# Reading the chunk state of a gated linear attention over all 112 rows at once, on one core

## The chip, the cores and the metric

One core of a Trainium2 chip runs the whole program. The metric is the device time of one execution in microseconds (us). The engines are named as in the profile: PE (matrix multiply), PEld (its weight loads), DVE (vector), ACT (scalar), POOL and SP (which here issues DMAs).

## The reference, cut to what matters

```
q, k, v, alpha: 4 batches x 8 heads x 768 tokens x 48, float32
state[d,e] = alpha_t[d] * state[d,e] + k_t[d] * v_t[e]        (per batch and head)
y_t[e]     = sum_d q_t[d] * state[d,e]
x   = y with the heads side by side: 4 x 768 x 384
u   = x + real(fft over tokens and over columns of x)
un  = layer norm of u over its 384 columns
out = u + relu(un @ w_ch1) @ w_ch2                            (384 -> 1536 -> 384)
```

## The kernel before

The recurrence is computed in chunks of 128 tokens, six to a sequence, and two heads at a time: a **pair** (16 of them, four to a batch). Within a pair the rows (partitions) 0 to 47 hold the 48 state rows of the first head and rows 64 to 111 those of the second; rows 48 to 63 are padding, so a pair takes 112 rows (`CW`). `HEADS` gives the two row slices, 0:64 and 64:112.

`attn_stages` writes the work of one pair as stages. s1 to s3 form running products of alpha and the scaled k and q on DVE. s4 transposes k on PE. s5 multiplies scaled q with scaled k per chunk and head on PE, with operands of 64 rows (first head) and 48 rows (second head), ACT copies the results out and POOL masks them; the result is `X`. s6 makes the contribution of each of the first five chunks to the state (`pu`, on PE), and DVE turns it into the state before each later chunk: one tensor_tensor over 112 x 240, then four dependent scalar_tensor_tensor of 112 x 48. They write the tile `tt`, one of two that alternate between pairs.

s7 makes the output of the six chunks. For chunk cc there is, for each head, a matmul of `X` with the values `vn` (128 rows; 64 streamed columns, of which 48 are used), called **V** here, and for cc > 0 a matmul of `e["A"]` with the state, called **T** here, which adds to the same columns. T runs over rows 0:64 for the first head and 64:112 for the second, with 48 streamed columns each. Each head has a PSUM bank of its own (`py[hd]`) for all six chunks; after chunks 2 and 5, ACT copies the three finished chunks of each head out (`FL["ev"].copy`, 128 x 144, four per pair). A matmul of plain float32 operands shows as two instructions in the trace (the 160 calls of T stand there as 320), one of the fp32r type as one.

After s7 the batch is combined over tokens, mixed by Fourier matrices, normed, and goes through the two layers of 384 -> 1536 -> 384, the **F** matmuls here (fp32r, 128 rows, 384 columns; 864 of each layer). The attention of batch b+1 is interleaved with the F matmuls of batch b. Batch 0's attention has no such work beside it.

The order on every engine is fixed ahead by a planner, `Plan.emit` (from line 363): it gives each operation a duration (`duration`), starts it when its inputs are ready by that account (matmuls other than F wait 0.8 us more, `MARGIN`), and takes, among what can start, what has the lowest key. PE executes strictly in the planned order. PSUM has eight banks: three "a" (attention and mixing), two "f1" and three "f2" (F matmuls); batch 0's attention may use all eight.

Up to a planned time of 120 us (`WARM`) the planner puts **fillers** into the planned gaps of PE (line 1135 in the profile): matmuls of a zero tile of 32 columns into columns 480:512 of bank 2 of "f2". It leaves them out while that bank holds an unfinished sum (`self.open`).

Of the kernel before, what the change touches and what calls it, by code (L numbers as in the profile page):

```python
# [17 lines left out]
ALU = mybir.AluOpType  # L18
AX = mybir.AxisListType

B, H, S, D = 4, 8, 768, 48
DM = H * D
DFF = 4 * DM
P = 128
NT = S // P
NP2 = H // 2
# [3 lines left out]
HM = DM // 2  # L30
CW = 112
GRP = 64
VW = NT * H // NP2 * D + GRP - D
VROW = 640
EVAC = 5000.0
NY = 5
# [17 lines left out]
KCK = -700.0  # L54
KF0 = -505.0
WARM = 120.0
MARGIN = 0.8
DUMMY = 0.11
KTINY = 0.5 * 2.0**15 / (1.0 + 15.5 / 128.0)
# [39 lines left out]
HEADS = ((0, slice(0, GRP)), (1, slice(GRP, CW)))  # L99
# [78 lines left out]
class Plan:  # L178


    def __init__(self, engines):
        self.engines, self.ops, self.tags, self.direct, self.key, self.chain, self.fill = engines, [], {}, None, 0.0, None, False
        self.idle, self.open, self.both, self.half = None, False, None, None

    def tag(self, name, count, make):
        reals = [make(i) for i in range(count)]
# [176 lines left out]
    def emit(self):  # L363
# [5 lines left out]
        clock = {e: 0.0 for e in self.engines}  # L369
# [6 lines left out]
        order = []  # L376
# [22 lines left out]
        while placed < len(ops):  # L399
            placed += 1  # L400
            best = None
            for e, cand in wait.items():
                if not cand:
                    continue
                now = clock[e]
                times = []
                for n in cand:
                    op = ops[n]
                    t = start(op, e)
                    if t is None:  # L410
                        continue
                    if len(op.engines) > 1:
                        if any(finish(op, o) < finish(op, e) - SLACK[e] for o in op.engines if o != e):
                            continue
                    times.append((t, max(now, t), n))
                if not times:
                    continue
                first = min(x[1] for x in times)
                key, n, t = min((ops[n].key, n, max(t, now)) for t, late, n in times if late <= first + WINDOW[e])
                if best is None or t < best[0]:  # L420
                    best = (t, n, e)
            assert best is not None, "no instruction can be placed"
            t, n, engine = best
            op = ops[n]
            for e in op.engines:
                wait[e].remove(n)
            op.engine, op.dur = engine, op.durs[engine]
            if engine == "PE":
                if op.half is not None and self.half is not None and op.half != self.half:
                    op.dur, self.half = 0.04, None  # L430
                else:
                    self.half = op.half
            for slot in op.slots:
                if slot.tag and slot.cell is None:
                    tag = self.tags[slot.tag]
                    slot.cell = tag["free"].pop(0)[1]
                    tag["taken"].add(slot.index)
                    while tag["next"] in tag["taken"]:
                        tag["next"] += 1
            if op.engine == "PE" and self.idle and t < self.idle[2] and not self.open:  # L440
                for _ in range(int((t - max(clock["PE"], self.idle[1])) / DUMMY)):
                    order.append(self.idle[0])
            if op.name == "matmul" and self.idle and (op.args[0].tile.tag, op.args[0].tile.cell) == self.idle[3]:
                self.open = not op.kwargs["stop"]
            if op.port and op.engine in held:
                op.dur += max(0.0, held[other[op.engine]] - t)
                held[op.engine] = t + op.dur
            end = t + op.dur
            clock[op.engine] = end
            if "dma" in op.name:  # L450
                dge = max(dge, t) + 0.45
                wire = max(wire, dge + 0.6) + op.wire
                end = wire + 1.0
            op.t, op.end = t, end
            order.append(n)
            for slot in op.slots:
                slot.touched.append(end)
                if slot.tag and len(slot.touched) == slot.uses:
                    tag = self.tags[slot.tag]
                    tag["free"].append((max(slot.touched) + 0.2, slot.cell))  # L460
                    tag["free"].sort(key=lambda x: x[0])
            for m in op.users:
                u = ops[m]
                u.left -= 1
                for e in u.engines:
                    lat = 0.0 if "dma" in op.name else LAT[op.engine][e]
                    if e == "PE" and op.engine != "PE" and not u.fill:
                        lat += MARGIN
                    u.ready[e] = max(u.ready[e], t if u.behind == n else end + lat)
                    if not u.left:  # L470
                        wait[e].append(m)
        self.order = [n for n in order if isinstance(n, int)]
        for n in order:
# [3 lines left out]
            op = ops[n]  # L477
# [21 lines left out]
def gla_mix_ffn(ctx: ExitStack, tc: tile.TileContext, alpha, kq, v, w1, w2, consts, rowtab, out):  # L499
    nc = tc.nc  # L500
    plan = Plan({"PE": nc.tensor, "ACT": nc.scalar, "DVE": nc.vector, "POOL": nc.gpsimd, "SP": nc.sync})
# [33 lines left out]
    def psa():  # L535
        if state["start"]:
            state["i"] += 1
            return plan.tile(start_tags[state["i"] % 8])
        return plan.tile("a")
# [8 lines left out]
    def fixed(shape, name, dtype=F32):  # L548
        return plan.fixed(cp.tile(shape, dtype, name=name))
# [3 lines left out]
    ident = cst[:, ID_O : ID_O + P]  # L553
    wts = [None] * (NW // 2)
    loaded = {}
    tts = [fixed([P, NT - 1, D], f"tt{i}") for i in range(2)]
    mts = [fixed([P, NT], f"mt{i}") for i in range(3)]
    d1 = fixed([P, S], "d1")
    back = fixed([P, S], "back")
# [4 lines left out]
    zero = fixed([P, 32], "zero")  # L564
# [47 lines left out]
    def setup():  # L612
        V.memset(zero, 0.0)
        V.memset(d1, 0.0)
        V.memset(back, 0.0)
        V.memset(back[:, C - 1 :: 2 * C], 1.0)
        V.memset(cm63, -63.0)
        V.memset(ceps, 1e-6)
        for x in mts:
            V.memset(x, 0.0)  # L620
        V.memset(ones, 1.0)
        V.memset(bad, 0.0)
# [40 lines left out]


    def attn_stages(b, hp, i, mixed):
        tt, mt = tts[i], mts[hp % 3]
        pair = b * NP2 + hp
        e = {}
        halves = "p (c h t) -> p c h t"
# [78 lines left out]
        def s6():  # L748
            pu = psa()
            for a in range(NT - 1):  # L750
                for hd, r in HEADS:
                    T.matmul(
                        pu[r, a * D : (a + 1) * D], e["kt"][:, a, r], loaded["vn", pair][:, (2 * a + hd) * D : (2 * a + hd + 1) * D],
                        start=True, stop=True,
                    )
            V.tensor_tensor(
                out=tt[0:CW], in0=pu[0:CW, 0 : (NT - 1) * D].rearrange("p (a e) -> p a e", e=D),
                in1=mt[0:CW, 0 : NT - 1, None].broadcast_to([CW, NT - 1, D]), op=ALU.mult,
            )
            for a in range(1, NT - 1):  # L760
                V.scalar_tensor_tensor(
                    out=tt[0:CW, a], in0=tt[0:CW, a - 1], scalar=mt[0:CW, a : a + 1], in1=tt[0:CW, a], op0=ALU.mult, op1=ALU.add,
                )

        def s7():
            X = e["X"]
            ytiles = mixed()[0]
            py = [psa() for _ in HEADS]
            for h2 in range(2):
                for c in range(3):  # L770
                    cc = 3 * h2 + c
                    cs = slice(cc * P, (cc + 1) * P)
                    o = cc * GRP
                    for hd, _ in HEADS:
                        T.matmul(
                            py[hd][:, o : o + GRP], X[h2][:, hd, c], loaded["vn", pair][:, (2 * cc + hd) * D : (2 * cc + hd) * D + GRP],
                            start=True, stop=cc == 0,
                        )
                    for hd, r in HEADS if cc else ():
                        T.matmul(py[hd][:, o : o + D], e["A"][r, cs], tt[r, cc - 1], start=False, stop=True)  # L780
                for hd, _ in HEADS:
                    yo = py[hd][:, 3 * h2 * GRP : 3 * (h2 + 1) * GRP].rearrange("p (a e) -> p a e", a=3)[:, :, 0:D]
                    FL["ev"].copy(ytiles[h2][:, :, (2 * hp + hd) * D : (2 * hp + hd + 1) * D], yo)

        return [s1, s2, s3, s4, s5, s6, s7, lambda: combine(*mixed(), hp * 2 * D, 2 * D, FL["comb"])]

# [343 lines left out]
    pf = psa()  # L1130
    T.matmul(pf[0:1, 0:1], bs, ones, start=True, stop=True)
    V.tensor_scalar_min(fl, pf[0:1, 0:1], 1.0)
    warm = plan.tags["f2"]["reals"]
    if WARM:
        plan.idle = (lambda: nc.tensor.matmul(warm[2][0:32, 480:512], zero.real(), zero.real(), start=True, stop=True), 1.0, WARM, ("f2", 2))  # L1135
    with tc.manual_schedule():
        plan.emit()

# [145 lines left out]
```

## Time and profile before

| | |
|---|---|
| three runs | 570.28, 576.63, 589.35 us (median 576.63) |
| the profiled execution | 578.74 us, of which the span of the trace is 577.0 us |
| mean granted PE clock in it | 0.93 |
| busy: PE, PEld, DVE, ACT, POOL | 555.3, 515.7, 341.6, 192.1, 77.5 us |

The stages overlap. Up to about 101 us there is batch 0's attention and mixing, with the splitting of the weights on ACT and DVE; from there the F matmuls are interleaved with the attention and mixing of the next batch, and from about 448 us on almost only F matmuls are left. The last F matmul ends at 569 us.

A row of a group of instructions gives line, engine, operation, out<-in by the names of tiles, shapes, count, total busy time and mean time of one in ns. For a matmul "64*128 64x48" is the weight tile (rows * columns) and the moving tile (rows x streamed columns). The names there are those of the pools: w is `e["A"]` or X, vn the values, f and a the PSUM banks, h, x and wt operands of the F matmuls. A row of the view by stretches of time gives the stretch, its length, the busy time and number of instructions of PE, PEld, DVE, ACT and POOL in it, the mean granted PE clock, the share of the DMA engines and GB/s. Line 481 is that of the planner's emission and so says nothing of the place in the code.

### The profile page before, as it was taken

The page shows a single profiled execution, that of the slowest core. Times are in us where ns is not written, and L with a number is a line of the kernel's source. Part 1 is how long each engine was busy: PE and PEld are TensorE (multiplying, and loading weights), DVE is VectorE, ACT ScalarE, POOL GpSimd, SP SyncE. Part 2 cuts the span into 40 slices and gives each one's busy share as a digit, 9 for nine tenths or more (in the row PEclk, how much of TensorE's full clock was granted, in tenths as well). Part 3 has the DMA queues.
Part 4 walks back from the last instruction along what each step waited for, and adds up shares of the span by engine and source line. Part 5 has one row for each costly group of instructions (what it writes and reads, how often), then busy time and mean ns, then how long its engine had stood idle before and what let it go on. Part 6 is the DMA issues. An engine that isn't in the chain of part 4 may idle for free.

```text
span 577.0 us, 11019 instructions
## 1 busy us (share of the span) xinstructions
PE 555.3 (96%) x4550; PEld 515.7 (89%) x4550; DVE 341.6 (59%) x831; ACT 192.1 (33%) x425; POOL 77.5 (13%) x99
## 2 busy tenths in 40 slices
PE   6999996999999999999999999999999999999995
PEld 5888895888788999988889999988889999999994
DVE  6986598797558599855326993456344931312211
ACT  2566356434255323532223241422222132211110
POOL 0212082034011200103112000013112000000000
PEclk9899598799789799998778999999989999999999
DMA  8980034020342501122225200101011100100101
GB/s 303 408 323 8 34 119 152 1 83 22 110 187 105 157 1 43 51 95 83 76 77 158 96 1 1 42 25 54 22 42 42 42 2 0 43 1 0 42 1 47
DMA packets 17130, 44.70 MB, mean 77 GB/s; under 512 B 1904, under 2 KB 7152, under 8 KB 17072
## 3 DMA queue, kind: packets, MB, share of 16 engines
q1 hardware_dynamic: 16016, 41.49, 20.3%
q0 software_dynamic: 768, 2.36, 1.5%
q8 instruction: 38, 0.62, 0.4%
q14 instruction: 20, 0.16, 0.1%
q10 hardware_dynamic: 288, 0.07, 0.1%
HBM read 36.83 MB, written 7.08 MB: 76 GB/s over the span
## 4 chain that ended last, share of the span: by engine, by line
PE 89%; DVE 5%; ACT 3%; DMA 2%; issue 1%; SPq 0%; ACTq 0%
PE f L481 59%; PE a L481 27%; PE f L1135 3%; DVE wt L481 1%; DMA al<-in_alpha_dram 1%; DVE y L481 1%; DVE z L481 1%; DMA wt<-in_w_dram 1%; ACT y L481 1%; SPq L481 0%; ACT L481 0%; DVE f L481 0%; ACT x L481 0%; ACT c L481 0%; ACT b L481 0%
## 5 line engine op out<-in xcount | busy, mean ns | idle before, releaser
L481 PE MATMUL f<-wt,h 128*128 128x384 f32 x864 | 186.7, 353 | 0.3 <-ACT h L214 0.3
L481 PE MATMUL f<-x,wt 128*128 128x384 f32 x864 | 184.9, 352 | 0.6 <-DVE h L481 0.6
L481 PEld LDWEIGHTS f<-x,wt 128*128 128x128 f32 x864 | 157.1, 195 | 2.9 <-DVE h L481 0.9
L481 PEld LDWEIGHTS f<-wt,h 128*128 128x128 f32 x864 | 155.7, 195 | 2.3 <-issue 0.7
L481 DVE SCALAR_TENSOR_TENSOR h<-f,h 128x384 fp32r<-128x384 f32 x96 | 53.2, 556 | 130.5 <-ACT h L214 129.7
L214 ACT ACTIVATE h<-f 128x384 fp32r<-128x384 f32 x96 | 47.1, 492 | 198.0 <-PE f L481 190.3
L481 POOL TENSOR_SCALAR_AFFINE_SELECT w<-w 128x384 f32<-128x384 f32 x48 | 35.3, 756 | 179.5 <-ACT w L481 179.5
L481 PE MATMUL a<-vn,w 128*128 128x64 f32 x288 | 47.7, 294 | 0.0
L1135 PE MATMUL f<-zero 128*32 128x32 f32 x956 | 41.3, 208 | 2.4 <-ACT x L481 1.2
L1135 PEld LDWEIGHTS f<-zero 128*32 128x32 f32 x956 | 37.9, 124 | 6.3 <-ACT x L481 2.1
L481 PEld LDWEIGHTS a<-vn,w 128*128 128x128 f32 x288 | 39.6, 200 | 3.6
L481 ACT COPY w<-a 128x384 f32<-128x384 f32 (+4 forms) x60 | 26.6, 481 | 37.8 <-PE a L481 37.7
L481 PEld LDWEIGHTS a<-tt,w 48*128 48x128 f32 (+1 forms) x290 | 26.9, 199 | 13.1 <-issue 5.7
L481 PE MATMUL a<-tt,w 48*128 48x48 f32 (+1 forms) x290 | 36.5, 304 | 1.2
L481 DVE TENSOR_TENSOR sd<-y,y 128x288 f32<-128x288 f32 x32 | 13.2, 453 | 39.3 <-ACT y L481 39.3
L481 ACT COPY y<-a 128x144 f32<-128x144 f32 x58 | 14.3, 280 | 56.9 <-PE a L481 55.0
L481 POOL DMA_INDIRECT y<-scr,rows x12 | 23.3, 1942 | 59.3 <-DMA scr<-y 44.6
L481 DVE TENSOR_TENSOR y<-y,a 128x191 f32<-128x191 f32 (+2 forms) x88 | 26.1, 344 | 8.0 <-PE a L481 8.0
L481 DVE TENSOR_TENSOR_SCAN w<-al,d 112x768 f32<-112x768 f32 (+1 forms) x17 | 28.4, 1673 | 3.5 <-POOL al L481 3.4
L481 PEld LDWEIGHTS a<-w,al 48*128 48x128 f32 (+1 forms) x306 | 22.9, 210 | 7.2 <-issue 5.4
L481 PE MATMUL a<-w,al 48*128 48x128 f32 (+1 forms) x306 | 28.4, 314 | 0.0
L481 DVE TENSOR_TENSOR_SCAN al<-al,back 112x768 f32<-112x768 f32 (+1 forms) x17 | 28.2, 1658 | 0.0
(116 smaller groups left out, 564.1 us busy)
## 6 DMA issues: line engine op xcount, KB each, us to landing
kq<-in_kq_dram SPq DMA_DIRECT2D x13, 768.0 KB, 5.7
wt<-in_w_dram SPq DMA_DIRECT2D x8, 768.0 KB, 4.6
al<-in_alpha_dram SPq DMA_DIRECT2D x15, 384.0 KB, 9.3
out_dram<-y SPq DMA_DIRECT2D x24, 192.0 KB, 1.9
vn<-in_v_dram SPq DMA_DIRECT2D x14, 296.0 KB, 2.8
wt<-in_w_dram SPq DMA_DIRECT2D x8, 384.0 KB, 4.6
scr<-y SPq DMA_DIRECT2D x4, 576.0 KB, 3.4
wt<-in_kq_dram SPq DMA_DIRECT2D x2, 768.0 KB, 9.6
```

The costliest lines, as they stand in the source:

```text
L214: return lambda out, x: e.activation(out, x, AF.Relu)
L481: op.ins = op.fns[op.engine](*[real(a) for a in op.args], **{k: real(x) for k, x in op.kwargs.items()})
L1135: plan.idle = (lambda: nc.tensor.matmul(warm[2][0:32, 480:512], zero.real(), zero.real(), start=True, stop=True), 1.0, WARM, ("f2", 2))
```

## The change

1. The state is kept for both heads in one tile `tt` of 112 rows x (5 x 2 x 48) that is zeroed once by POOL. DVE computes the state as before, but in a tile `tc_`; two ACT copies then put the first head's rows into its columns and the second head's rows into its own. Thus the blocks off the diagonal stay zero, and one T over rows 0:112 with 96 streamed columns gives both heads. There is one `tt` and one `tc_` for all pairs, where there were two `tt`.
2. V streams 80 columns of `vn` in place of 64 (`NV`); the values are loaded 16 columns wider.
3. Both heads of three chunks share one PSUM bank (3 x 2 x 80 = 480 columns); the second three chunks take another one. ACT copies 128 x 288 out of each, two per pair in place of four. Columns 480:512 stay free for fillers.
4. Fillers go to the first bank of f2, then f1, that holds no unfinished sum; before, only bank 2 of f2 was used.
5. The planner's account of a matmul on 64 rows or fewer is changed: 0.03 us where a second-head matmul follows a first-head one, and 0.09 us more (`SWITCH`) where the order goes between such matmuls and those on more rows.

```diff
-VW = NT * H // NP2 * D + GRP - D
+NV = 80
+VW = NT * H // NP2 * D + NV - D
+SWITCH = 0.09
...
             if engine == "PE":
-                if op.half is not None and self.half is not None and op.half != self.half:
-                    op.dur, self.half = 0.04, None
-                else:
-                    self.half = op.half
+                if op.half == GRP and self.half == 0:
+                    op.dur = 0.03
+                elif (op.half is None) != (self.half is None):
+                    op.dur += SWITCH
+                self.half = op.half
...
-            if op.engine == "PE" and self.idle and t < self.idle[2] and not self.open:
-                for _ in range(int((t - max(clock["PE"], self.idle[1])) / DUMMY)):
-                    order.append(self.idle[0])
-            if op.name == "matmul" and self.idle and (op.args[0].tile.tag, op.args[0].tile.cell) == self.idle[3]:
-                self.open = not op.kwargs["stop"]
+            if op.engine == "PE" and self.idle and t < self.idle[2]:
+                bank = next((x for x in self.idle[3] if x not in self.open), None)
+                if bank:
+                    order.extend([lambda bank=bank: self.idle[0](*bank)] * int((t - max(clock["PE"], self.idle[1])) / DUMMY))
+            if op.name == "matmul":
+                bank = op.args[0].tile.tag, op.args[0].tile.cell
+                (self.open.discard if op.kwargs["stop"] else self.open.add)(bank)
...
-    tts = [fixed([P, NT - 1, D], f"tt{i}") for i in range(2)]
+    tts = [fixed([P, NT - 1, 2, D], f"tt{i}") for i in range(1)]
+    tc_ = fixed([P, NT - 1, D], "tc")
...
+        for x in tts:
+            G.memset(x, 0.0)
...
             V.tensor_tensor(
-                out=tt[0:CW], in0=pu[0:CW, 0 : (NT - 1) * D].rearrange("p (a e) -> p a e", e=D),
+                out=tc_[0:CW], in0=pu[0:CW, 0 : (NT - 1) * D].rearrange("p (a e) -> p a e", e=D),
...
             for a in range(1, NT - 1):
...(the same four operations, on tc_ in place of tt)
+            for hd, r in HEADS:
+                A.copy(tt[r, :, hd], tc_[r])
...
-            py = [psa() for _ in HEADS]
             for h2 in range(2):
+                py = psa()
                 for c in range(3):
                     cc = 3 * h2 + c
                     cs = slice(cc * P, (cc + 1) * P)
-                    o = cc * GRP
-                    for hd, _ in HEADS:
+                    o = c * 2 * NV
+                    for hd in range(2):
                         T.matmul(
-                            py[hd][:, o : o + GRP], X[h2][:, hd, c], loaded["vn", pair][...: (2 * cc + hd) * D + GRP],
-                            start=True, stop=cc == 0,
+                            py[:, o + hd * NV : o + (hd + 1) * NV], X[h2][:, hd, c], loaded["vn", pair][...: (2 * cc + hd) * D + NV],
+                            start=hd == 0, stop=cc == 0 and hd == 1,
                         )
-                    for hd, r in HEADS if cc else ():
-                        T.matmul(py[hd][:, o : o + D], e["A"][r, cs], tt[r, cc - 1], start=False, stop=True)
-                for hd, _ in HEADS:
-                    yo = py[hd][:, 3 * h2 * GRP : 3 * (h2 + 1) * GRP].rearrange("p (a e) -> p a e", a=3)[:, :, 0:D]
-                    FL["ev"].copy(ytiles[h2][:, :, (2 * hp + hd) * D : (2 * hp + hd + 1) * D], yo)
+                    if cc:
+                        yo = py[:, o : o + 2 * NV].rearrange("p (h e) -> p h e", h=2)[:, :, 0:D]
+                        T.matmul(yo, e["A"][0:CW, cs], tt[0:CW, cc - 1], start=False, stop=True)
+                yo = py[:, 0 : 6 * NV].rearrange("p (a h e) -> p a h e", a=3, h=2)[:, :, :, 0:D]
+                FL["ev"].copy(ytiles[h2][:, :, hp * 2 * D : (hp + 1) * 2 * D].rearrange("p a (h e) -> p a h e", h=2), yo)
```

More of the change, by code (lines that the diff above doesn't have):

```diff
@@ L182, in __init__ @@
         self.engines, self.ops, self.tags, self.direct, self.key, self.chain, self.fill = engines, [], {}, None, 0.0, None, False
-        self.idle, self.open, self.both, self.half = None, False, None, None
+        self.idle, self.open, self.both, self.half = None, set(), None, None
     def tag(self, name, count, make):
@@ L665, in attn_stages @@
     def attn_stages(b, hp, i, mixed):
-        tt, mt = tts[i], mts[hp % 3]
+        tt, mt = tts[0], mts[hp % 3]
         pair = b * NP2 + hp
@@ L761, in s6 @@
                 V.scalar_tensor_tensor(
-                    out=tt[0:CW, a], in0=tt[0:CW, a - 1], scalar=mt[0:CW, a : a + 1], in1=tt[0:CW, a], op0=ALU.mult, op1=ALU.add,
+                    out=tc_[0:CW, a], in0=tc_[0:CW, a - 1], scalar=mt[0:CW, a : a + 1], in1=tc_[0:CW, a], op0=ALU.mult, op1=ALU.add,
                 )
+            for hd, r in HEADS:
+                A.copy(tt[r, :, hd], tc_[r])
         def s7():
@@ L772, in s7 @@
                     cs = slice(cc * P, (cc + 1) * P)
-                    o = cc * GRP
-                    for hd, _ in HEADS:
+                    o = c * 2 * NV
+                    for hd in range(2):
                         T.matmul(
-                            py[hd][:, o : o + GRP], X[h2][:, hd, c], loaded["vn", pair][:, (2 * cc + hd) * D : (2 * cc + hd) * D + GRP],
-                            start=True, stop=cc == 0,
-                        )
-                    for hd, r in HEADS if cc else ():
-                        T.matmul(py[hd][:, o : o + D], e["A"][r, cs], tt[r, cc - 1], start=False, stop=True)
-                for hd, _ in HEADS:
-                    yo = py[hd][:, 3 * h2 * GRP : 3 * (h2 + 1) * GRP].rearrange("p (a e) -> p a e", a=3)[:, :, 0:D]
-                    FL["ev"].copy(ytiles[h2][:, :, (2 * hp + hd) * D : (2 * hp + hd + 1) * D], yo)
+                            py[:, o + hd * NV : o + (hd + 1) * NV], X[h2][:, hd, c], loaded["vn", pair][:, (2 * cc + hd) * D : (2 * cc + hd) * D + NV],
+                            start=hd == 0, stop=cc == 0 and hd == 1,
+                        )
+                    if cc:
[3 more added lines that the diff above has]
+                FL["ev"].copy(ytiles[h2][:, :, hp * 2 * D : (hp + 1) * 2 * D].rearrange("p a (h e) -> p a h e", h=2), yo)
         return [s1, s2, s3, s4, s5, s6, s7, lambda: combine(*mixed(), hp * 2 * D, 2 * D, FL["comb"])]
@@ L1132, in gla_mix_ffn @@
     V.tensor_scalar_min(fl, pf[0:1, 0:1], 1.0)
-    warm = plan.tags["f2"]["reals"]
+    warm = {tag: plan.tags[tag]["reals"] for tag in ("f2", "f1")}
     if WARM:
-        plan.idle = (lambda: nc.tensor.matmul(warm[2][0:32, 480:512], zero.real(), zero.real(), start=True, stop=True), 1.0, WARM, ("f2", 2))
+        plan.idle = (
+            lambda tag, i: nc.tensor.matmul(warm[tag][i][0:32, 480:512], zero.real(), zero.real(), start=True, stop=True), 1.0, WARM,
+            [(tag, i) for tag in warm for i in reversed(range(len(warm[tag])))],
+        )
     with tc.manual_schedule():
```

## The prediction, made before the change was run

> **What bounds the kernel now.** I read the page's head first, then its chain, then the view by stretches of time, then the waits.
>
> ```profile
> span 577.0 us, 11019 instructions
> PE 555.3 (96%) x4550; PEld 515.7 (89%) x4550; DVE 341.6 (59%) x831; ACT 192.1 (33%) x425; POOL 77.5 (13%) x99
> PEclk9899598799789799998778999999989999999999
> PE 89%; DVE 5%; ACT 3%; DMA 2%; issue 1%; SPq 0%; ACTq 0%
> 56.00:73.00 17.00, 16.64 (x167) 14.97 (x167) 10.13 (x34) 5.28 (x12) 0.00 (x0) 0.50 0.14 40
> 107.20:151.50 44.30, 43.57 (x355) 38.84 (x354) 35.93 (x65) 17.98 (x43) 11.22 (x13) 1.00 0.19 56
> 151.50:568.00 416.50, 415.14 (x2794) 389.93 (x2794) 219.60 (x554) 119.02 (x276) 39.61 (x56) 0.95 0.16 53
> PEld a L481 <- DVE tt L481: 0.7, 3, 0.2
> ```
>
> PE is busy for 415.1 of 416.5 us from 151.5 us on, and 89% of the chain is PE. The last row is from the view of waits after 107 us: PE stands for the state tile 0.7 us in all. So from 107 us to 568 us time is PE's own work, and it falls only if PE's instructions need less of it. Two things in it aren't arithmetic: the granted clock (0.95 of full over that stretch), and what PE loses between instructions. Before 107 us the bound changes from engine to engine.
>
> **T, taken apart.** This is the view in order of time, from where s7 runs without F matmuls (start, length, line and operation, count).
>
> ```profile
> 283.28 0.28 PE L481 MATMUL a<-vn,w 128*128 128x64 f32 x1
> 283.39 0.46 PE L481 MATMUL a<-cst,al 112*128 112x112 f32 x3
> ...
> 284.32 0.43 PE L481 MATMUL a<-tt,w 64*128 64x48 f32 x4
> 284.67 0.66 PE L481 MATMUL a<-vn,w 128*128 128x64 f32 x4
> 285.26 0.42 PE L481 MATMUL a<-tt,w 64*128 64x48 f32 x4
> 285.62 0.66 PE L481 MATMUL a<-vn,w 128*128 128x64 f32 x4
> 286.42 0.64 PE L481 MATMUL a<-tt,w 64*128 64x48 f32 x4
> 286.99 0.66 PE L481 MATMUL a<-vn,w 128*128 128x64 f32 x4
> ```
>
> One chunk (four T, four V instructions) goes from 284.32 to 285.26: 0.94 us. A V is followed by a 112-row transpose after 0.11 us (283.28 to 283.39), so 112 rows after 128 cost no pause, and 0.11 is one instruction's slot where a full weight tile of 128 columns is loaded. Four V at that rate would take 0.45; they take 0.59 from their start to the next T. The rest lies where 64-row and 128-row work meet.
>
> After: two T instructions of 112 rows in place of four, all eight boundaries gone, six slots of 0.11: 0.67 us. Saving 0.27 a chunk. The bounds of the new T: its 96 columns are fewer than 128, and
>
> ```profile
> 439.38 5.29 PE a L481 x52
> 497.18 71.85 PE f L481 x408
> ```
>
> the Fourier matmuls of up to 128 columns, written with strides, run at 0.10 each, so I expect neither the gap in T's output nor the 80 columns of V to exceed the slot: 80/128 of 0.10 is 0.06. At worst T costs what its four take now, 0.36: no saving but the V boundaries.
>
> From 107 us there are 12 pairs of 5 such chunks: 60 x 0.27 = **16 us**. In the row at 286.42 the second half of the pair waits for ACT to empty the bank it shares with the first half: V to T is 0.80 instead of 0.64, and T to V 0.57 instead of 0.36, 0.37 in all. The second half gets its own bank now. For 12 pairs that is at most 4.4; together 16 to 21, **20 us** taken.
>
> **The clock.** The row at 0.95 says that (1 - 0.95) x 416.5 = 21 us of full-speed time are lost after 151.5 (rounding: 19 to 23), though PE is never idle there. Cut at the clock's steps (a fall and the stretch ahead of it, then a stretch that no fall follows):
>
> ```profile
> 284.66:288.08 3.42, 3.28 (x27) 2.83 (x26) 0.56 (x1) 0.62 (x3) 0.00 (x0) 1.00 0.00 0
> 288.08:294.90 6.82, 6.82 (x33) 5.51 (x33) 2.27 (x10) 1.67 (x5) 0.99 (x2) 0.50 0.45 162
> 410.96:414.37 3.41, 3.27 (x27) 2.70 (x27) 1.50 (x5) 1.33 (x4) 0.08 (x1) 1.00 0.01 2
> 414.37:417.78 3.41, 3.41 (x28) 2.86 (x28) 0.58 (x2) 0.71 (x3) 0.00 (x0) 1.00 0.00 0
> ```
>
> What PE issued in the first and in the third of these, by form:
>
> ```profile
> L481 PE MATMUL a<-vn,w 128*128 128x64 f32 x13 | 2.3, 294 | 0.0
> L481 PE MATMUL a<-tt,w 48*128 48x48 f32 x7 | 1.5, 287 | 0.0
> L481 PE MATMUL a<-tt,w 64*128 64x48 f32 x7 | 1.5, 287 | 0.1
> ...
> L481 PE MATMUL a<-vn,w 128*128 128x64 f32 x11 | 1.8, 284 | 0.0
> L481 PE MATMUL a<-tt,w 64*128 64x48 f32 x6 | 1.3, 290 | 0.1
> L481 PE MATMUL a<-tt,w 48*128 48x48 f32 x4 | 0.8, 290 | 0.0
> L481 PE MATMUL f<-wt,h 128*128 128x384 f32 x2 | 0.5, 336 | 0.0
> L481 PE MATMUL a<-cst,al 112*128 112x112 f32 x3 | 0.5, 261 | 0.0
> L481 PE MATMUL f<-x,wt 128*128 128x384 f32 x1 | 0.4, 419 | 0.0
> ```
>
> The first stretch is followed by half clock, the third isn't. Busy time doesn't separate them (3.28 and 3.27); streamed columns do. From the two rows above an F instruction streams 384 columns in 0.176 us and a float32 one 128 in 0.10. Then 284.66 holds 13 x 0.05 for V and 7 x 0.04 for T (two heads side by side count once), 0.93 of 3.42: 27%. 410.96 holds 0.55 + 0.24 + 3 x 0.09 + 3 x 0.176 = 1.6: 46%. So, an inference from these two: a stretch that streams somewhere under 46% is answered with half clock. A dense chunk before streams 4 x 0.05 + 2 x 0.04 = 0.28 of 0.94, 30%; after, 4 x 0.063 + 2 x 0.075 = 0.40 of 0.67, 60%. I forecast that s7 no longer trips it: all **21 us** come back; the lower bound is none.
>
> The Trainium skill, in "TensorE: Matmul & The Clock Gate", section "Why this matters for your kernels", ties the fall of the clock to PE-idle gaps of more than about 3 us. By that, 288 to 295 shouldn't have been slow; the row with 3.28 of 3.42 us busy speaks against it.
>
> **What is added.** Durations of the nearest rows:
>
> ```profile
> L481 DVE SCALAR_TENSOR_TENSOR tt<-tt,mt x64: 244/263/522, 19.3 to 422.9; 112x48 f32<-112x48 f32 x64
> L481 DVE TENSOR_TENSOR tt<-a,mt x15: 376/408/409, 27.8 to 421.3; 112x240 f32<-112x240 f32 x15
> L481 ACT COPY y<-a 128x144 f32<-128x144 f32 x58 | 14.3, 280 | 56.9 <-PE a L481 55.0 <-PE f L481 1.9
> L481 ACT COPY kt<-a 128x336 f32<-128x336 f32 x14 | 6.1, 437 | 15.0 <-PE a L481 13.3 <-PE f L481 1.7
> L481 ACT COPY d<-al 112x12 f32<-112x12 f32 x15 | 3.2, 212 | 1.5 <-DVE w L481 1.5
> L481 ACT ACTIVATE wt<-wt 128x768 f32<-128x768 f32 x9 | 7.6, 849 | 2.1 <-DVE wt L481 1.9
> ```
>
> The two ACT copies of 240 columns lie between 0.21 (12 columns) and 0.85 (768): 0.40 each, 32 of them, 13 us. The copies out fall from 64 x 0.28 to 32 of 288 columns, between 0.28 and 0.44: 0.40, 5 us less. ACT gets 8 us of work in its 385 idle ones: nothing on the path. The new wait is T's: the first T needed only the tensor_tensor (0.41), now it needs that, 4 x 0.26 and both copies, 2.3 us. Behind a waiting T stands all of PE. The planner knows these operations and puts F matmuls ahead; I take nothing, and 2.2 x 12 = 26 us where that cover is gone. The single tile `tt` holds up the next pair's copies until this pair's last T; on the page DVE and ACT have the room. The memset is POOL's, once, with POOL 13% busy: nothing. The wider value load and the altered SWITCH only shift the plan.
>
> **Before 107 us.** At half clock throughout, the chain is PE from 57 to 69, then DVE:
>
> ```profile
> 59.30 4.54 PE f L481 x20
> ...
> 69.87 0.83 DVE sd L481 x2
> 97.39 0.90 PE L481 MATMUL f<-cst,f 128*128 128x128 f32 x3 [4.82 <-ACT f L481]
> ```
>
> Those 20 instructions of s7 take 4.54 us. At full clock, without boundaries, the last pair's s7 would need some 6 us less, but its state tile is late too: DVE finishes it among weight splitting, and the copies come behind weight work of 0.85 on ACT. I take **4 us**, bounds 0 and 10. From 70 to 97 DVE, ACT and a load lead; nothing there is removed. The new banks for fillers matter only here: a filler that is planned too long stands ahead of real work in PE's order (loss up to 6), one that fills the 4.82 us gap could save the half clock after it (gain up to 5). Left at nothing.
>
> **Sum**, against the profiled execution: 578.7 - 20 - 21 - 4 = **533.7**. It is 2 above the median of the runs, 576.6; since what spreads the runs (570 to 589) is most likely that clock, I don't shift the sum: 533.
>
> **The rivals.**
> - *The clock stays as it is*: 578.7 - 20 - 4 = 555. For it: only windows with F are seen staying up, none of float32 alone at 60%. Against: 46% sufficed. The page's idle-gap rule leads here too. 0.12.
> - *T saves nothing*: the two heads' T start side by side now (four within 0.36), and two in a row may cost that. 578.7 - 21 - 4 = 554, less the V boundaries. Against: the 112-row transposes at 0.11. "TensorE: Matmul & The Clock Gate", Part 3, of the Trainium skill says that small-row matmuls in different row groups run concurrently; by it, joining them gains nothing. 0.07.
> - *T waits* (slower): in s7 PE stands for the two copies in ACT's queue. From 2.2 us a pair on, 26 us eat the 20 saved, and 2.2 of 3.4 us idle streams under 46%, so each of 12 pairs earns 6.8 us at half clock, 41 lost: 578.7 - 20 + 26 - 21 + 41 = 605. It decides where the copies land more than `MARGIN`, 0.8 us, behind plan. Against: 0.7 us of waits for the state now. 0.04.
> - *The early stage goes another way*: fillers or copies delay it, 543; or both early slow spells go, 522. 0.15 together.
> - *The fillers' part does nothing*: then 533 still.
>
> **How the numbers follow.** Forecast 0.62. The range takes in 522 with some room, the two 554s: 516 to 557; outside are the wait and several misses at once. A change of under 2% can hardly be told from none here: below 565 is faster, 0.94; 565 to 588 the same, 0.04 (half of it the two 554s coming together, 578.7 - 4 = 575, half a wait of T that is only partly exposed); slower 0.02, the rest of that wait.
>
> **What would show it.** T: 112-row groups of two, V to V at 0.11 across them, s7 chunks at 0.67. Clock: 1.00 in all stretches from 107 us to the end. Copies: 0.40, and next to no PE waits for ACT or tt. It is wrong if stretches at 0.50 stay beside 60% streaming, or if PE idles ahead of T.

## The result, and the profile after

The changed kernel takes 529.26 us in the median, the kernel before 581.51 in the four runs of it on record here: a ratio of 0.9215 with a 95% interval of 0.908 to 0.935. The executions of the kernel before scatter with the granted clock, 570 to 589 us here, and this ratio and those of the experiments compare the fast ones alone, here 528.4 with 573.5 us in the mean. The forecast was 533. One of the four executions of the changed kernel took 1672.69 us; it counts in the median but not in the ratio, and its cause isn't known; none of the later kernels showed such a run.

The head of the profile after, its view by stretches of time and its waits from 100 us on:

```profile
span 527.1 us, 10743 instructions
PE 507.7 (96%) x4414; PEld 487.5 (92%) x4414; DVE 343.7 (65%) x835; ACT 201.9 (38%) x424; POOL 71.5 (14%) x97
PEclk9799977899999999999999999999999999999998
107.20:151.50 44.30, 44.30 (x360) 42.21 (x357) 38.23 (x76) 24.97 (x49) 7.94 (x13) 1.00 0.40 139
151.50:516.00 364.50, 363.36 (x2563) 352.83 (x2562) 210.64 (x531) 114.93 (x256) 36.37 (x52) 1.00 0.15 51
ACT tt L486 <- DVE tc L486: 4.8, 4, 1.4
```

The granted clock is 1.00 in both stretches where it was 1.00 and 0.95. PE still is the bound (363.4 of 364.5 us), and the longest wait around the new state tiles is ACT's for DVE, 4.8 us in all; no row has PE waiting for `tt`.

Where the 50 us of span went can be read from three moments: the first F instruction, the end of the last one, the end of the span. First the kernel before, then the changed one, from the views in order of time and of the chain:

```profile
102.73 1.01 PE L481 MATMUL f<-x,wt 128*128 128x384 f32 x2
559.90 9.13 PE f L481 x52
```

```profile
92.57 1.01 PE L486 MATMUL f<-x,wt 128*128 128x384 f32 x2
447.20 71.85 PE f L486 x408
92.57:107.20 14.63, 14.63 (x134) 12.96 (x132) 12.09 (x23) 6.17 (x14) 1.22 (x3) 0.89 0.01 1
```

F work starts at 92.57 instead of 102.73: **10.2 us** from the early stage. From there to the end of the last F it was 569.03 - 102.73 = 466.3 us and is 519.05 - 92.57 = 426.5: **39.8 us** less. The clock's part: before, (1 - 0.95) x 416.5 = 21 (22 when the half-clock stretches are added up at their steps) and some 2 more between 102.7 and 107.2, at 0.50; after, (1 - 0.89) x 14.63 = 1.6. This counts half of the time at half clock as lost. So 21 to 23 us are the clock's in this execution of the kernel before, and the other 17 to 19 us are PE's work with fewer slots and boundaries.

An s7 of the changed kernel without F matmuls, from its first T on:

```profile
229.80 0.36 PE L486 MATMUL a<-tt,w 112*128 112x96 f32 x2
229.99 0.60 PE L486 MATMUL a<-vn,w 128*128 128x80 f32 x4
230.43 0.62 PE L486 MATMUL a<-tt,w 112*128 112x96 f32 x4
230.89 0.60 PE L486 MATMUL a<-vn,w 128*128 128x80 f32 x4
231.32 0.40 PE L486 MATMUL a<-tt,w 112*128 112x96 f32 x2
231.56 0.60 PE L486 MATMUL a<-vn,w 128*128 128x80 f32 x4
231.99 0.40 PE L486 MATMUL a<-tt,w 112*128 112x96 f32 x2
232.32 0.94 PE L486 MATMUL a<-w,al 64*128 64x128 f32 x12
```

From V to V (230.89 to 231.56) and from T to T (231.32 to 231.99) a chunk takes 0.67 us, where it took 0.94. No gap stands between the halves of the pair. One boundary is left: the T at 231.99, the last of this s7, are followed by the 64-row work of another pair's s5.

### The profile page after: what moved, and what is told of

Same layout as the page of the kernel before. It is cut to its first block, busy times and chain, and to the rows that moved or that the text cites. A ratio compares the mean times of both kernels' runs of the same rounds, so it can differ in the third digit from the quotient of the medians.

```text
span 527.1 us, 10743 instructions
## 1 busy us (share of the span) xinstructions
PE 507.7 (96%) x4414; PEld 487.5 (92%) x4414; DVE 343.7 (65%) x835; ACT 201.9 (38%) x424; POOL 71.5 (14%) x97
## 4 chain that ended last, share of the span: by engine, by line
PE 86%; issue 4%; POOL 3%; DMA 2%; ACT 2%; DVE 1%; SPq 0%; ACTq 0%; POOLq 0%
PE f L486 60%; PE a L486 23%; PE f L1146 3%; POOL y L486 2%; DMA al<-in_alpha_dram 1%; DMA wt<-in_w_dram 1%; DVE y L486 1%; SPq L486 0%; ACT x L486 0%; POOL x L486 0%; POOL wt L486 0%; DVE al L486 0%; ACT L486 0%; ACT c L486 0%; ACT h L216 0%
## 5 line engine op out<-in xcount | busy, mean ns | idle before, releaser
L486 PE MATMUL f<-x,wt 128*128 128x384 f32 x864 | 179.4, 345 | 0.2 <-ACT x L486 0.2
L486 PE MATMUL f<-wt,h 128*128 128x384 f32 x864 | 178.1, 343 | 0.3 <-ACT h L216 0.3
L486 PEld LDWEIGHTS f<-wt,h 128*128 128x128 f32 x864 | 150.5, 188 | 2.9 <-issue 0.5
L486 PEld LDWEIGHTS f<-x,wt 128*128 128x128 f32 x864 | 151.3, 189 | 1.3 <-ACT x L486 0.5
L486 PE MATMUL a<-vn,w 128*128 128x80 f32 x288 | 43.9, 272 | 0.0
L486 POOL DMA_INDIRECT y<-scr,rows x12 | 21.8, 1819 | 54.0 <-DMA scr<-y 36.4
L486 PE MATMUL a<-tt,w 112*128 112x96 f32 x144 | 26.0, 278 | 0.0
L486 DVE TENSOR_TENSOR y<-y,f 128x384 f32<-128x384 f32 (+2 forms) x46 | 20.6, 479 | 7.4 <-PE f L486 7.3
L486 PE MATMUL a<-w,al 48*128 48x128 f32 (+1 forms) x306 | 24.2, 288 | 0.0
L486 PEld LDWEIGHTS a<-w,al 48*128 48x128 f32 (+1 forms) x306 | 19.5, 187 | 4.6 <-ACT w L486 2.2
L486 ACT COPY y<-a 128x288 f32<-128x288 f32 x29 | 11.5, 397 | 29.6 <-PE a L486 29.6
```

Source lines behind the costliest of these rows:

```text
L486: op.ins = op.fns[op.engine](*[real(a) for a in op.args], **{k: real(x) for k, x in op.kwargs.items()})
```

## The experiments

**E1: the clock alone.** If the clock follows what PE streams, it must come back without any change to T.

```diff
 (before)
-VW = NT * H // NP2 * D + GRP - D
-VROW = 640
+NV = 128
+VW = NT * H // NP2 * D + NV - D
+VROW = 704
...
-    py[hd][:, o : o + GRP], X[h2][:, hd, c], loaded["vn", pair][...: (2 * cc + hd) * D + GRP],
+    py[hd][:, o : o + NV], X[h2][:, hd, c], loaded["vn", pair][...: (2 * cc + hd) * D + NV],
```

> The kernel before, with one change: V streams 128 columns in place of 64 (the values are loaded wider), the split T untouched; an instruction with a weight load of 128 columns takes 0.11 us either way. Theory A, the clock follows streamed columns: a dense chunk streams 4 x 0.10 + 2 x 0.04 = 0.48 of 0.94 us, 51%, over the 46% that was seen to hold; the stretches at 0.50 after 107 us go and 21 to 23 us come back with no T saved, and the one from 56 to 73 us may go too (up to 6 more): a span of 548 to 556 from 577. Theory B, the clock falls because of the switches between 64-row and 128-row work or because of the number of instructions: as before, about 577, and stretches at 0.50 inside s7 stay.

Measured: 552.66 us in the median, 0.972 (0.968 to 0.975) of the kernel before; the span of the profile 551.5. Its clock and its stretches:

```profile
PEclk9999997899999999999999999999999999999999
56.00:73.00 17.00, 14.26 (x287) 13.29 (x286) 14.87 (x35) 7.26 (x14) 6.96 (x2) 1.00 0.23 71
107.20:151.50 44.30, 43.55 (x360) 38.09 (x360) 34.90 (x70) 18.89 (x45) 12.45 (x15) 1.00 0.23 71
151.50:540.00 388.50, 387.14 (x2703) 364.50 (x2702) 214.89 (x540) 114.02 (x265) 39.21 (x54) 1.00 0.17 56
94.70 1.01 PE L482 MATMUL f<-x,wt 128*128 128x384 f32 x2
```

One of its clock's steps that holds s7 alone, by form, with the step behind it:

```profile
277.03:280.45 3.42, 3.27 (x26) 2.68 (x28) 0.00 (x0) 0.50 (x2) 0.00 (x0) 1.00 0.00 0
280.45:283.86 3.41, 3.41 (x24) 3.18 (x25) 1.19 (x3) 0.94 (x3) 0.00 (x0) 1.00 0.35 103
L482 PE MATMUL a<-vn,w 128*128 128x128 f32 x12 | 2.1, 300 | 0.0
L482 PE MATMUL a<-tt,w 48*128 48x48 f32 x7 | 1.6, 292 | 0.0
L482 PE MATMUL a<-tt,w 64*128 64x48 f32 x7 | 1.6, 292 | 0.1
```

This is nearly the step of the kernel before at 284.66, which had 13 V and the same 14 T instructions and was followed by half clock. Only V's columns differ: 12 x 0.10 + 7 x 0.04 = 1.5 of 3.42 us streamed, 43% in place of 27%, and the clock stays at 1.00. The split T with its eight boundaries is untouched, and no half-clock stretch is left after 107 us. Streaming columns that nobody reads gained 25 us of span between the two profiles: theory B falls. By the ratio it is some 16 us: the clock of the kernel before was 0.930 in its profile and up to 0.953 in other executions, where less is lost, while all four of E1 had 0.988 or 0.989. The columns aren't quite free: a chunk takes 1.00 us from T to T (276.89 to 277.89) instead of 0.94, 3.6 us over 60 chunks. The early stage gained too: F starts at 94.70, 8.0 us sooner than in the kernel before, with 56 to 73 us at 1.00 instead of 0.50.

**E2: T in full rows, but little streaming.** The other half of the same question, in the changed kernel.

```diff
 (after)
-NV = 80
+NV = 48
...
-    yo = py[:, o : o + 2 * NV].rearrange("p (h e) -> p h e", h=2)[:, :, 0:D]
-    T.matmul(yo, e["A"][0:CW, cs], tt[0:CW, cc - 1], start=False, stop=True)
+    for hd in range(2):
+        T.matmul(
+            py[:, o + hd * NV : o + hd * NV + D], e["A"][0:CW, cs], tt[0:CW, cc - 1, hd], start=False, stop=hd == 1
+        )
```

> The changed kernel, with V streaming 48 columns and T as two matmuls of 112 rows and 48 columns, one for each head, in place of one of 96 columns. No 64-row work is left in s7, but a dense chunk is eight slots of 0.11 and streams 8 x 0.0375 = 0.30 of 0.90 us, 33%. Theory A (streamed columns): 120 more T slots cost 13 us and the half-clock stretches come back at the pairs without F matmuls, some 15 to 21 us: 555 to 563 from 529. Theory B (the row switches): the clock stays at 1.00 and only the slots cost: 542.

Measured: 564.46 us in the median (561.07 to 570.1), 0.991 (0.983 to 0.999) of the kernel before. The view in order of time, the forms in the clock's step ahead of a fall, and the stretches:

```profile
154.86 0.77 PE L486 MATMUL a<-tt,w 112*128 112x48 f32 x6
155.47 0.61 PE L486 MATMUL a<-vn,w 128*128 128x48 f32 x4
155.91 0.83 PE L486 MATMUL a<-tt,w 112*128 112x48 f32 x6
156.58 0.61 PE L486 MATMUL a<-vn,w 128*128 128x48 f32 x4
157.03 0.61 PE L486 MATMUL a<-tt,w 112*128 112x48 f32 x4
157.47 0.61 PE L486 MATMUL a<-vn,w 128*128 128x48 f32 x4
```

```profile
L486 PE MATMUL a<-tt,w 112*128 112x48 f32 x19 | 2.8, 274 | 0.0
L486 PE MATMUL a<-vn,w 128*128 128x48 f32 x12 | 1.8, 275 | 0.0
L486 PE MATMUL f<-x,wt 128*128 128x384 f32 x2 | 0.5, 338 | 0.0
```

```profile
158.22:171.88 13.66, 13.66 (x79) 12.50 (x79) 6.86 (x19) 4.38 (x9) 2.22 (x4) 0.50 0.23 81
171.88:264.04 92.16, 90.46 (x684) 86.41 (x683) 68.94 (x167) 36.12 (x80) 13.28 (x18) 1.00 0.24 79
264.04:267.45 3.41, 3.41 (x12) 3.41 (x12) 1.34 (x3) 0.59 (x2) 0.12 (x1) 0.50 0.00 0
```

Half clock is back in a kernel whose s7 has no 64-row work at all. The step from 154.81 to 158.22 streams 31 x 0.0375 + 2 x 0.176 = 1.5 of 3.41 us, 44%, and is followed by a fall; the two F instructions in this count had started before the step, and without them it is 34%. With E1 this settles it for these kernels: the row split isn't what lowers the clock. The size was less than theory A said: two falls after 107 us (17 us at half clock, 8.5 lost), not 15 to 21, and the second, at 264.04, isn't of this kind, for PE stood idle for 1.4 us of the step ahead of it, waiting for POOL. The rest of the difference from the changed kernel is the T slots and an early stage in which the clock fell as well, with F from 104.24 us on; so the median is 1.5 us above A's range.

E2 also takes T's saving apart. At full clock its chunk of eight full-row slots takes 0.89 us (from V to V, 156.58 to 157.47), where the split T took 0.94 and the joined T takes 0.67: nearly all of the saving comes from one T for both heads, and little from the rows alone.

**E3 and E4: 64 and 48 columns instead of 80.** `NV = 64` and `NV = 48`, nothing else.

> The changed kernel with V streaming 64 columns as before, in place of 80. Theory A: a dense chunk streams 4 x 0.05 + 2 x 0.075 = 0.35 of 0.67 us, 52%, over 46%: no stretch at 0.50 after 100 us, 529 as with 80. Rival: the 80 columns are what holds the clock, and half-clock stretches come back, up to 20 us more.

> The changed kernel with V streaming the 48 columns that are used. A dense chunk streams 4 x 0.0375 + 2 x 0.075 = 0.30 of 0.67 us, 45%. Theory A puts the limit between 41% or so (a fall followed) and 46% (none followed), so this places the limit: if the clock stays, it is under 45% and the time is 529; if it falls, it is above, and some 7 to 20 us come on top. Rival: columns don't matter, 529 and 1.00 throughout.

Measured: 525.77 us (ratio 0.925, 0.916 to 0.934) and 526.23 us (0.927, 0.920 to 0.934), the same as with 80 as far as these runs tell. E4's stretches and one of its s7:

```profile
107.00:515.00 408.00, 406.91 (x2899) 394.60 (x2898) 249.43 (x608) 140.32 (x305) 39.29 (x61) 1.00 0.17 57
226.68 0.86 PE L486 MATMUL f<-wt,h 128*128 128x384 f32 x4
227.37 0.36 PE L486 MATMUL a<-tt,w 112*128 112x96 f32 x2
...
228.46 0.57 PE L486 MATMUL a<-vn,w 128*128 128x48 f32 x4
228.86 0.43 PE L486 MATMUL a<-tt,w 112*128 112x96 f32 x2
229.13 0.57 PE L486 MATMUL a<-vn,w 128*128 128x48 f32 x4
229.53 0.43 PE L486 MATMUL a<-tt,w 112*128 112x96 f32 x2
229.89 0.94 PE L486 MATMUL a<-w,al 64*128 64x128 f32 x12
```

So the 80 columns aren't needed once T has 112 rows and 96 columns. E4 doesn't place the limit as its text hoped: s7 between two denser pieces is only 227.37 to 229.89, 2.5 us, shorter than one of the clock's steps of 3.41, so no step consists of s7 alone. In the kernel before, the dense stretch went from 284.3 past 289 us; in E2 it is 154.86 to 158.6. That it is the shortness that keeps the clock up at 45% in s7 is argued and not shown: no run has a longer s7 at that share. E4 also writes T's 96 columns without a gap, and its chunk takes the same 0.67 us (228.46 to 229.13) as with the gap of 32. The Trainium skill's page "PSUM — Partial Sum Buffer", section "Specifications (TRN2)", says that any non-contiguous access pattern slows matmuls significantly; for two runs of 48 columns the two chunks of 0.67 us don't bear that out.

**E5, E6, E7: the planner's parts.** E5 is the changed kernel with fillers in bank 2 of f2 only; E6 the changed kernel with the old account of 64-row matmuls; E7 the kernel before with both new planner parts.

```diff
 (E5, after)
-            [(tag, i) for tag in warm for i in reversed(range(len(warm[tag])))],
+            [("f2", 2)],
 (E6, after; E7, before, the other way, with the new rule of the fillers)
-                if op.half == GRP and self.half == 0:
-                    op.dur = 0.03
-                elif (op.half is None) != (self.half is None):
-                    op.dur += SWITCH
-                self.half = op.half
+                if op.half is not None and self.half is not None and op.half != self.half:
+                    op.dur, self.half = 0.04, None
+                else:
+                    self.half = op.half
```

> The changed kernel with the fillers' old rule: only bank 2 of f2, left out while that bank holds an unfinished sum. Theory A: the earlier start of the F matmuls (92.6 us instead of 102.7) comes from the clock that s7 itself holds up and from shorter s7 work, so it stays within 3 us: 526 to 533. Rival: it comes from the fillers in other banks, then F starts near 102 us again and the time is 536 to 540.

> The changed kernel with the planner's old account of 64-row matmuls (0.04 us where the head changes, no SWITCH). The instructions are the same, only the planned order and the planned gaps shift. Theory A: nothing in the sum hangs on it, 525 to 533. Rival: with the shorter planned times PE is late against the plan and waits for ACT's copies of the state or of X, 535 or more, with PE waits for tt or w in the view of waits.

> The kernel before with both planner parts of the change (fillers in any bank with no unfinished sum, the new account with SWITCH) and none of the parts in s7. Theory A: the clock still falls in s7 after 107 us and the four T instructions stay, so no gain beyond the scatter of the kernel before: a span of 567 to 580. Rival: the planner parts carry the early gain, 10 us less.

Measured: E5 526.71 us (0.927, 0.920 to 0.934), E6 526.23 (0.926, 0.918 to 0.934): neither part carries any of the gain in the changed kernel. In E5 the fillers are even the same in number, 980 instructions. E7 takes 567.74 us, 0.991 (0.986 to 0.997) of the kernel before. Its falls after 107 us are three single steps:

```profile
157.74:161.15 3.41, 3.41 (x14) 3.33 (x13) 2.72 (x10) 1.20 (x3) 0.00 (x0) 0.50 1.01 402
287.45:290.86 3.41, 3.41 (x13) 3.41 (x12) 1.84 (x8) 0.46 (x2) 0.00 (x0) 0.50 0.81 248
400.09:403.50 3.41, 3.41 (x19) 2.75 (x18) 1.84 (x8) 1.20 (x5) 0.12 (x1) 0.50 0.00 0
```

That is 10 us at half clock instead of 44 in the profiled execution of the kernel before. Whether the shifted order avoids falls isn't shown by this: the mean clock of the kernel before lay between 0.908 and 0.953 from one execution to the next, that of E7 between 0.926 and 0.953. F starts where it did, at 102.8. So theory A held for the early stage and in the comparison of runs; its range for the span was missed (562.1, under 567). The rival's 10 early us aren't there.

**E8: fillers packed more closely.** The changed kernel with `NV = 64` and `DUMMY = 0.08`.

> The changed kernel with V of 64 columns and 0.08 in place of 0.11 us as the planned length of a filler, so that planned gaps before 120 us hold 37% more of them (two instructions of 0.035 us each are 0.07). Theory: the half-clock stretches near 65 to 72 and 86 to 96 us come after gaps in which the fillers ran out; with them filled the F matmuls start 2 to 4 us earlier, 521 to 525. Rival: the fillers stand ahead of real work in PE's order, 526 to 532.

Measured: 526.13 us (0.923, 0.919 to 0.928), as E3, and not the 521 to 525 of the theory. There are more fillers, as asked, and they gain nothing:

```profile
L1146 PE MATMUL f<-zero 128*32 128x32 f32 x1340 | 50.2, 199 | 2.8 <-DVE zero L486 1.0 <-ACT x L486 0.8 <-issue 0.7
56.00:107.00 51.00, 48.39 (x895) 44.82 (x894) 46.43 (x115) 29.57 (x54) 14.47 (x11) 1.00 0.33 110
94.34 0.69 PE L1146 MATMUL f<-zero 128*32 128x32 f32 x16 [0.79 <-ACT x L486]
94.96 0.61 PE L486 MATMUL f<-x,wt 128*128 128x384 f32 x2
```

The clock is at 1.00 from 56 to 107 us, and the first F starts at 94.96, later than the 92.57 of the changed kernel and the 91.15 of E3, whose clock was 0.90 from 56 us on: ahead of it PE waits for ACT's `x`. So raising the early clock from 0.90 to 1.00 is worth nothing here, while raising it from 0.50 went with 8.0 us in E1. Why F starts later than in E3 was not separated. No variant beats the changed kernel by more than the runs can tell.

## Why the prediction was right, point by point

- **PE as the bound after about 100 us**: held; busy 363.4 of 364.5 us.
- **T, 20 us (16 to 21)**: the chunk is 0.67 as worked out, the 112-row T takes one slot. Measured 17 to 19 for the whole. E1 gives the same by another way: from the first F to the end of the last it takes 449.1 us, of which 2.4 go to half clock before 99.5 us, and the changed kernel 426.5 with 1.6; that is 21.8 us between them, and 3.6 of it is the wider V. What was too large is the wait between the halves, taken at all 12 pairs: in the view in order of time it stands at 8 of them, and the others had F work there. The reading was off the other way too: four V usually take 0.59 to the next T, not 0.64, so the wait is 0.42, 3.4 us for 8 pairs in place of 4.4. Of the boundaries, the one from s7 to s5 stays.
- **The clock, 21 us**: 21 to 23, and E1 and E2 show the mechanism as inferred from two stretches. What the prediction put wrongly is why s7 no longer trips it: it gave 60% streaming over 46%, with the 80 columns in the sum. E3 and E4 show that the columns of V don't matter there, beside 96 columns in T and a shorter s7. The limit of 46% isn't established either. The count takes whole instructions that began before the step, and their F moves it by 10%: E2's fall is at 44% with them and at 34% without. And E2 has a step of 43%, with no F in it, that no fall follows (287.93 to 291.34: 26 instructions of 48 columns and five pairs of 128, 1.5 of 3.41 us). What the traces show is that a step of s7 alone was followed by half clock at 27% in the kernel before and not at 43% in E1; where between them the limit lies, and whether there is one figure, is open.
- **The early stage, 4 us (0 to 10)**: 10.2, the mis-sized term, just past its upper bound. It was thought that DVE and ACT would eat most of what s7 gains from 57 to 69 us. E1 got 8.0 with the split T as it was, and the clock at 1.00 from 56 to 73 us. That the fillers were worth nothing (E5) was the prediction's value.
- **What was added**: ACT's copies into `tt` and out of the shared bank were taken at 0.40 each, and POOL's memset at nothing:

```profile
L486 ACT COPY tt<-tc 64x240 f32<-64x240 f32 x16 | 6.3, 391 | 6.0 <-DVE tc L486 5.7
L486 ACT COPY tt<-tc 48x240 f32<-48x240 f32 x16 | 6.2, 389 | 0.3
L486 ACT COPY y<-a 128x288 f32<-128x288 f32 x29 | 11.5, 397 | 29.6 <-PE a L486 29.6
L486 POOL MEMSET tt<- 128x480 f32 x1 | 0.5, 497 | 0.3 <-POOLq L1287 0.3
```

- **The rivals**: "the clock stays" fell with the granted clock of 1.00 after 107 us; "T saves nothing" with the chunk of 0.67; "T waits" with the view of waits, in which PE never waits for the state. That wait was not provoked by an experiment, so how much room it has is open.

The Trainium skill's rule on the clock ("TensorE: Matmul & The Clock Gate", section "Why this matters for your kernels": no PE-idle gaps of more than about 3 us between matmuls) doesn't cover the falls after 107 us in the kernel before: in the steps ahead of them PE was busy for 3.27 us or more of 3.41. The fall at 97 us there does follow an idle gap, of 4.82 us.

## What to carry to other kernels

Read the granted clock beside the busy share: a PE that is 96% busy with short matmuls, whose slot of 0.11 us is the same for 48, 64 or 80 streamed columns, can still be slowed to half. The remedy here was more streamed columns in each of the clock's steps, by fuller matmuls (the changed kernel) or by columns nobody needs (E1); keeping such a piece shorter than a step may be another, which E4 suggests. Where small matmuls for two groups of rows alternate with full ones, price the boundaries from starts to starts, not from the mean duration; a zero-blocked operand over all rows can cost less than the pair it replaces. Fillers that hold the clock are worth something only where PE is the next bound; in E8 it wasn't.

## What was not expected of the hardware

Widening V from 64 to 128 streamed columns, a pure waste of work, made the kernel 25 us faster in the span (577.0 to 551.5), and some 16 by the ratio of the runs. And half clock came with next to no idle time (3.28 of 3.42 us busy), in steps of 3.41 us, ahead of which PE streamed 27% (before) or 34 to 44% (E2) of the time.
